# Second layer norm of a sequence-mixing and feed-forward kernel: epsilon on GpSimd, ten of sixteen normalizations as one ScalarE pass, under a new written order

## The chip, the cores and the metric

The kernel runs on one core of a Trainium2 chip. A core has five instruction queues that run side by side and wait for each other through semaphores: PE (TensorE, matrix products and transposes), DVE (VectorE), ACT (ScalarE), POOL (GpSimd) and SP (SyncE, which here only issues DMAs). PEld is TensorE's loading of weights. Each queue works strictly in its own order: an instruction that waits holds up all that stands behind it on the same engine.

The metric is the device time of one execution in microseconds (us). The profile tells of the span, from the first to the last instruction, which is a little shorter.

## The reference

The input x is 2048 tokens by 640 channels. The first half is a long convolution with gates, around the normalized x; the second is a feed-forward block with the Mish activation on the normalized result of the first.

```python
x = A_q
h  = x + _A_ref(_layernorm(x), A_k, A_v, A_shift_k, A_ssm_k, A_ssm_D)
h2 = h + _B_ref(_layernorm(h), B_w1, B_b1, B_w2)

# _A_ref(q, k, v, ...):
#   k_shift = causal convolution of k with 4 taps per channel
#   kv      = k_shift * v
#   y       = causal convolution of kv with ssm_k (2048 taps per channel, by FFT) + kv * ssm_D
#   return q * y
# _B_ref(x, w1, b1, w2):           # 640 -> 1728 -> 640
#   hid = x @ w1 + b1
#   return (hid * tanh(softplus(hid))) @ w2
```

`_layernorm` subtracts the mean over the 640 channels and divides by the root of the variance plus 1e-5.

## The kernel before, in words

The long convolution is done as a transform in two stages written as matrix products. The work is cut into named operations, and each stage writes a PSUM buffer (there are four of them, `ps0` to `ps3`) which ACT or DVE then evicts, that is copies to SBUF as bf16:

- `d_n`, `d_k`, `d_v`, `d_g`, `d_x`: loads of the filter, k, v, the table G and x (q), in pieces. `dadd` adds `ssm_D` to the filter's first tap.
- `k1pe`/`k1ev`: transposes of the filter; `s1kpe`/`s1kev`: first stage of the transform of the filter, 20 tiles; `s2kpe`/`s2kev`: second stage, 22 tiles.
- `ktpe`/`ktev`/`ktsh`: transposes of k and a shift by one; `kspe`: the four-tap convolution, ten tiles; `kv`: the product with v, on DVE from PSUM.
- `s1v`, `s2v`: the two stages for kv. `sw`: a copy of the filter's transform with pairs of partitions swapped, by DMA. `pr`: product of both transforms on DVE, 20 pieces.
- `i1pe`/`i1ev`: first inverse stage, 20 tiles; `i2a`, `i2b`, `i2pe`: second inverse stage, one tile of 128 tokens each (16 tiles), evicted by `y`.

Then each of the 16 token tiles goes through the gate and the two layer norms:

- `ln1_` (DVE, lines 506 to 510): statistics of x; `ln1p` (POOL): epsilon, power -0.5 and minus mean times that; `lnx` (ACT or POOL): the normalized x in one pass.
- `wb` (DVE): y times the normalized x; `h` (DVE): plus x, in place.
- `bn` (DVE, lines 540 to 545): statistics of h, and in a last small instruction the variance plus epsilon (`ve2`, line 544); `pow` (POOL, line 546): `ve2` to the power -0.5, `r2`; `hc` (DVE, lines 547 and 548): h minus mean, times `r2`, one instruction over 128 by 640.
- `tr`: the transpose of hc into the layout of the feed-forward block: on PE for tiles 0 and 1 (`trpe`, evicted by `trev`), by a transposing DMA on SP's queue for the others.

The feed-forward block works on units of 2, 2, 4, 4 and 4 token tiles. `m1pe{unit}_{0..6}` are the first products (line 586, and 593 for the last half chunk), `hb` the Mish pass on ACT (line 608), `m2pe` the second products (line 651), `res` the addition of h (DVE, line 676), `d_out` the store on SP's queue. Units 0 and 1 share their second products, which wait for all their `hb`.

The order of the operations on every queue is not found at run time: it is the text `ORDER` (lines 26 to 61), emitted token by token. `@2` says which PSUM buffer an operation of PE writes, `:a`, `:d` and `:p` override the engine (ACT, DVE, POOL). An operation of PE that takes a PSUM buffer waits until the eviction of its last user is done. All DMAs marked as loads, swaps, transposes and stores stand on SP's queue in this order too.

Of the kernel before, what the change touches and what calls it, by code (L numbers as in the profile page):

```python
# [30 lines left out]
ktpe4_1 ktpe1_0@0 ktpe1_1 ktpe1_3 d_g3 ktpe1_2 ktpe4_2 ktev1:a ktpe0_0@2 ktev4 ktpe0_2 ktpe0_1 ktpe2_0@1 d_g0 ktpe0_3 ktpe2_2 ktev0 s1kpe4_3@3 d_g5
s1kpe4_1@0 s1kev4_3 ktpe2_3 s1kev4_1:d ktsh0 ktpe3_0@2 ktpe3_1 d_g6 ktsh1 ktpe3_3 ktpe3_2 ktpe2_1 ktsh4 ktev3 kspe0_0@3 ktev2:a wsh1 d_g4 kspe0_1@0
kv0_0 s1kpe2_3@2 s1kpe4_2@1 kv0_1 s1kev2_3 ktsh3 kspe4_1@3 ktsh2 s1kev4_2 s1kpe3_1@2 kv4_1 s1vpe0_2@0 s1kev3_1 s1kpe2_1@1 s1vev0_2:d s1vpe0_1@3
s1kev2_1 kspe1_1@2 s1vev0_1 s2kpe_36@0 kv1_1 s2kpe_114@1 s2kev_36 kspe3_0@3 s2kev_114:d s2kpe_24@2 kspe1_0@0 s2kev_24 kv3_0 s2kpe_18@1 s2kpe_12@2
s2kev_18 kv1_0 kspe4_0@3 s2kev_12 s2kpe_90@1 kv4_0 s2kpe_54@0 s2kev_90 kspe3_1@2 s2kev_54 s2kpe_60@3 kv3_1 s1vpe0_3@1 s2kev_60 s2kpe_78@0 kspe2_1@2
s1vev0_3 s2kev_78:d s2kpe_102@3 s2kpe_0@1 kv2_1 s2kev_102 kspe2_0@0 s2kev_0 s2kpe_66@3 d_x3 kv2_0 s1vpe1_3@2 s2kev_66 s1vpe3_2@1 s1vev1_3:d d_x1
s1vpe3_0@0 s1vev3_2 s1vpe1_1@3 d_x0 d_x2 s1vev3_0 s1vev1_1:d s1vpe0_0@2 s2kpe_120@1 s1vev0_0 s1vpe2_2@0 s2kev_120:d s1vpe1_2@3 s1vev2_2 s1vpe2_0@2
s1vev1_2:d s1vpe1_0@1 s1vev2_0 s2kpe_6@0 d_t2m s2kpe_72@3 s1vev1_0 s2kev_6:d s2kpe_48@2 s2kev_72 s2kpe_96@1 s2kev_48:d s2v0pe_16@0 s2kev_96 s2kpe_84@3
s2v0ev_16:d s2kpe_30@2 s2kev_84 s1vpe4_2@1 ln1_3 s2kev_30 s2kpe_42@0 s2kpe_126@3 s2kev_42 s2kev_126:d s2kpe_108@2 ln1p3 ln1_0 s1vpe4_1@3 s2kev_108
s1vpe4_0@0 s1vev4_1:d s1vev4_2 ln1p0 s1vpe4_3@2 sw0_0 sw0_1 s1vev4_0 s1vev4_3:d s1vpe2_3@1 sw3_0 s1vpe3_3@3 lnx3:p s1vev2_3 sw1_1 s1vpe3_1@0  # L40
s1vev3_3:d s1vpe2_1@2 sw4_1 s1vev3_1 s2v0pe_0@1 lnx0:p sw2_1 ln1_1 s2v0pe_96@3 s1vev2_1 sw1_0 s2v0pe_80@0 sw3_1 ln1_2 s2v0ev_96 ln1p1 s2v0pe_64@2
sw2_0 s2v0ev_80 s2v0ev_0:d sw4_0 s2v0pe_32@3 lnx1:p s2v0ev_64 s2v0pe_112@0 pr0_0 ln1p2 s2v0pe_48@1 s2v0ev_112 s2v2pe_0@2 s2v0ev_32:d lnx2:p s2v0ev_48
s2v2pe_112@0 pr0_64 s2v2ev_112 s2v2pe_80@3 s2v1pe_64@1 s2v2ev_0 pr0_96 s2v2ev_80 s2v2pe_96@0 pr0_32 s2v2pe_32@2 s2v2ev_96 s2v2pe_64@3 pr1_96 s2v2ev_64
s2v2pe_16@0 pr1_64 s2v2ev_32 i1pe0_0@3 s2v1ev_64 s2v2pe_48@2 pr1_32 s2v2ev_48 i1pe0_3@1 pr1_0 s2v2ev_16 s2v1pe_0@2 pr3_32 i1ev0_0 s2v1pe_96@0 i1ev0_3
pr3_96 s2v1pe_32@3 s2v1ev_0 pr3_64 i1pe0_2@1 d_w12 s2v1ev_32 d_w11 i1pe0_1@2 pr4_96 d_w10 i1ev0_2 d_w13 i1pe1_2@3 pr3_0 d_w14 i1ev0_1 i1pe1_3@1
i1ev1_2 pr2_64 i1pe1_0@2 s2v1ev_96 pr2_0 i1pe3_0@3 i1ev1_3 i1pe3_2@0 pr2_32 i1ev1_0 i1pe3_1@1 pr4_64 i1ev3_0 i1pe3_3@2 i1ev3_1 pr2_96 i1pe1_1@3
# [4 lines left out]
hc2 pow3 y9 m1pe0_1@0 ln1_12 tr2 y5 w2z hb0_0 m1pe0_4@1 hc3 wb9 ln1p5 tr3 hb0_1 wb4 m1pe0_2@2 hb0_4 ln1_11 ln1p8 lnx5 m1pe0_5@3 wb7 hb0_2 ln1p12
ln1_10 m1pe0_6@0 hb0_5 m1pe1_6@1 h4 ln1p11 lnx12 ln1_15 m1pe1_0@2 hb1_6 ln1p10 ln1_14 lnx11 m1pe1_3@3 bn4 hb0_6 ln1p15 hb1_0 m1pe1_5@1 hb1_3 wb5
m1pe1_2@0 h7 hb1_5 wb6 h6 m1pe1_4@2 lnx15:p hb1_2 bn7 pow4 m1pe1_1@3 hb1_4 h5 pow7 hc4 i2pe11@1 bn6 hb1_1 ln1p14 tr4 i2pe12@0 m2pe0@2 y12 h9 lnx14:p
hc7 lnx10 bn9 pow6 y11 lnx8 hc6 pow9 bn5 tr6 m2pe2@3 wb14 pow5 tr7 hc9 wb10 wb11 tr9 wb8 hc5 h10 tr5 h8 wb15 bn8 m2pe1@0 h11 pow8 bn10 hc8 pow10 res0
m1pe2_6@1 h15 d_out0 ln1_13 tr8 m1pe2_1@2 hc10 ln1p13 hb2_6 res2 tr10 bn11 lnx13:p m1pe2_3@3 h14 hb2_1 pow11 wb12 hc11 h12 tr11 bn15 m2pe3@1 hb2_3
d_out2 wb13 pow15 bn14 hc15 pow14 bn12 tr15 m1pe3_6@2 h13 pow12 bn13 m1pe2_0@3 hc14 pow13 hb3_6 res3 res1 d_out3 hc12 d_out1 m1pe2_4@1 hc13 tr14 hb2_0
tr13 m1pe3_4@2 hb2_4 tr12 m1pe2_2@0 hb3_4 m1pe3_1@3 hb2_2 m1pe3_5@1 hb3_1 m1pe2_5@2 m1pe3_3@0 hb2_5 m1pe3_0@3 hb3_3 hb3_5 m1pe3_2@2 hb3_0 m2pe5@0
hb3_2 m2pe7@1 m2pe4@3 res7 res5 d_out7 d_out5 m2pe6@2 m1pe4_0@1 res6 res4 d_out4 d_out6 m1pe4_2@0 hb4_0 m1pe4_6@2 m1pe4_1@3 hb4_6 hb4_2 m1pe4_3@1
# [110 lines left out]
def kernel(  # L169
# [333 lines left out]
    for t in range(NT):  # L503
# [36 lines left out]
        def bnf(e, t=t):  # L540
            for hh in range(2):
                nc.vector.bn_stats(st2[:, t, hh, :], xt(t)[:, hh * 320:(hh + 1) * 320])  # L542
            nc.vector.bn_aggr(mv2[:, t, :], st2[:, t, :, :])
            nc.vector.tensor_scalar(ve2[:, t:t + 1], mv2[:, t, 1:2], EPS, None, ALU.add)  # L544
# [1 line left out]
        o_pw = OP(f"pow{t}", "pool", [o_bn, o_small], emit=lambda e, t=t: nc.gpsimd.tensor_tensor(r2[:, t:t + 1], ve2[:, t:t + 1], mhalf[:], ALU.pow))  # L546
        o_hc = OP(f"hc{t}", "dve", [o_pw] + ([trs[t - 7]] if t >= 7 else list(ks_pes.values())),
                  emit=lambda e, t=t: nc.vector.tensor_scalar(hc_s[t % 7], xt(t), mv2[:, t, 0:1], r2[:, t:t + 1], ALU.subtract, ALU.mult))
# [173 lines left out]
```

## Time and profile before

| | us |
|---|---|
| median of three executions | 226.48 (226.25 to 226.64) |
| profiled execution | 226.59 |
| its span | 224.7 |
| PE busy | 214.4 (95%) |
| DVE busy | 137.6 (61%) |
| ACT busy | 131.6 (59%) |
| POOL busy | 58.5 (26%) |

The busy shares are means over stages that differ: up to about 100 us, DVE and ACT are busy nearly all the time; from about 117 us on they have little to do, and PE has no gap. The granted clock of TensorE is full throughout. In the profile a line of the timeline gives the start, the duration, the engine, the source line, the operation, the tile written and the tiles read, how many in a row, and in brackets the idle time ahead of it and what ended that. `ks`, `uv`, `ra`, `rb`, `rw` and `G` are the big SBUF areas, which are used for several things one after another; `ps` is PSUM.

### The profile page before, as it was taken

What the parts mean: (1) busy time and instruction counts of PE and PEld (TensorE: products, weight loads), DVE (VectorE), ACT (ScalarE), POOL (GpSimd) and SP (SyncE); (2) the same over time, 40 slices, a digit from 0 to 9 for tenths busy, and PEclk for the clock granted to TensorE, in tenths of its full rate; (3) what the DMA queues carried; (4) which work ended last, traced back from release to release, by engine and by line L of the source; (5) the groups of instructions that cost most, each with busy time, mean ns of one, the idle gap of its engine ahead of it and who ended that gap; (6) DMA issues with size and microseconds to landing.
All of it is one profiled execution on the core that took longest, in us unless ns stands there. A gap on an engine that the chain in (4) does not pass through costs nothing.

```text
span 224.7 us, 6128 instructions
## 1 busy us (share of the span) xinstructions
PE 214.4 (95%) x2644; PEld 157.3 (70%) x2650; DVE 137.6 (61%) x250; ACT 131.6 (59%) x178; POOL 58.5 (26%) x106
## 2 busy tenths in 40 slices
...
GB/s 177 386 414 416 417 369 16 139 340 276 417 417 18 274 125 158 254 0 58 5 29 76 59 98 67 128 18 0 3 0 58 40 21 0 0 20 29 88 29 73
DMA packets 19563, 30.98 MB, mean 138 GB/s; under 512 B 10704, under 2 KB 14928, under 8 KB 18768
## 3 DMA queue, kind: packets, MB, share of 16 engines
...
q10 hardware_dynamic: 336, 0.12, 0.3%
...
## 4 chain that ended last, share of the span: by engine, by line
PE 65%; DVE 11%; ACT 10%; DMA 6%; POOL 3%; issue 2%; SPq 0%; DVEq 0%; POOLq 0%
PE ps L651 26%; PE ps L586 22%; ACT uv L259 8%; DVE ks L459 6%; DMA rb<-in_A_q_dram 4%; PE ps L394 3%; DMA ks<-in_A_ssm_k_dram 2%; PE ps L339 2%; PE ps L355 2%; PE ps L420 2%; PE ps L374 2%; PE ps L356 2%; PE ps L395 1%; PE ps L593 1%; PE ps L659 1%
## 5 line engine op out<-in xcount | busy, mean ns | idle before, releaser
L608 ACT ACTIVATE ks<-ps,b1s 128x512 bf16<-128x512 f32 (+1 forms) x69 | 36.2, 599 | 47.9 <-PE ps L586 30.7
L651 PE MATMUL ps<-ks 128*128 128x320 bf16 (+2 forms) x420 | 58.6, 299 | 0.0
L586 PE MATMUL ps<-G 128*128 128x512 bf16 (+1 forms) x319 | 57.5, 336 | 0.8 <-ACT ks L608 0.5
L651 PEld LDWEIGHTS <-ks 128*128 128x128 bf16 x420 | 40.6, 98 | 17.4 <-issue 1.3
L586 PEld LDWEIGHTS <-G 128*128 128x128 bf16 x325 | 31.2, 98 | 25.3 <-issue 1.3
L259 ACT CAST uv<-ps 128x1024 bf16<-128x1024 f32 x49 | 45.7, 1099 | 0.1
L676 DVE TENSOR_TENSOR rb<-ps,rb 128x640 bf16<-128x640 f32 x15 | 11.8, 820 | 50.5 <-PE ps L659 48.1
L259 ACT CAST ks<-ps 128x960 bf16<-128x960 f32 (+2 forms) x46 | 37.7, 912 | 7.9 <-PE ps L395 5.9
L459 DVE TENSOR_TENSOR ks<-ks,uv 128x2048 bf16<-128x2048 bf16 x20 | 23.4, 1239 | 0.0
L420 PEld LDWEIGHTS <-G 128*128 128x128 bf16 x512 | 20.6, 96 | 3.6 <-issue 2.9
L477 PE MATMUL ps<-a_t,ks 128*128 128x128 bf16 x320 | 19.0, 219 | 0.9 <-ACT uv L259 0.5
L477 PEld LDWEIGHTS <-ks 128*128 128x128 bf16 x320 | 18.4, 113 | 1.5 <-issue 0.5
L513 POOL TENSOR_SCALAR ve<-mv 128x1 f32<-128x1 f32 x16 | 4.6, 289 | 47.7 <-DVE mv L509 46.7
L546 POOL TENSOR_TENSOR r<-ve,mhalf 128x1 f32<-128x1 f32 x16 | 10.8, 675 | 16.9 <-DVE ve L544 16.8
L420 PE MATMUL ps<-uv,G 128*128 128x64 bf16 (+1 forms) x384 | 12.7, 186 | 1.7 <-ACT uv L259 1.3
L508 DVE BATCH_NORM_STATS2 st<-rb 128x6 f32<-128x320 bf16 x32 | 13.8, 472 | 0.8 <-DMA rb<-in_A_q_dram 0.8
L542 DVE BATCH_NORM_STATS2 st<-rb 128x6 f32<-128x320 bf16 x32 | 14.0, 480 | 0.1
L261 DVE CAST ks<-ps 128x1024 bf16<-128x1024 f32 (+2 forms) x12 | 13.2, 1127 | 1.4 <-PE ps L395 0.7
L261 DVE CAST uv<-ps 128x1024 bf16<-128x1024 f32 x11 | 13.1, 1205 | 0.1
L673 DVE TENSOR_TENSOR rb<-ps,rb 128x384 bf16<-128x384 f32 (+1 forms) x2 | 1.0, 492 | 19.9 <-PE ps L651 19.9
L360 DVE TENSOR_TENSOR ra<-ps,rb 128x1024 bf16<-128x1024 f32 x10 | 11.9, 1219 | 1.3 <-PE ps L356 0.7
L522 POOL TENSOR_SCALAR ra<-rb,r,nmr 128x640 bf16<-128x640 bf16 x10 | 12.1, 1212 | 1.2 <-PE ps L395 0.6
...
## 6 DMA issues: line engine op xcount, KB each, us to landing
...
```

Source lines behind the costliest of these rows:

```text
L259: nc.scalar.copy(o, i)
L261: nc.vector.tensor_copy(o, i)
L360: nc.vector.tensor_tensor(kv_w[:, m, :, 8 * h:8 * h + 8, :], p_.f32().rearrange("p (l t d) -> p d t l", l=4, t=8), raw_v[:, 8 * h:8 * h + ...
L420: nc.tensor.matmul(p_.f32()[:, o:o + n], g_v[:, f, :], src[:, :, f, :], start=True, stop=True)
L459: nc.vector.tensor_tensor(o, o, v, ALU.mult)
L477: nc.tensor.matmul(pz[:, dgl, :], KS[:, k, b, :, l], a12[:, k, :], start=k == 0, stop=k == 1)
L508: nc.vector.bn_stats(st1[:, t, hh, :], xt(t)[:, hh * 320:(hh + 1) * 320])
L522: nc.gpsimd.tensor_scalar(lnx_s[t % 9], xt(t), r1[:, t:t + 1], nmr1[:, t:t + 1], ALU.mult, ALU.add)
L542: nc.vector.bn_stats(st2[:, t, hh, :], xt(t)[:, hh * 320:(hh + 1) * 320])
L586: nc.tensor.matmul(ph[:, o:o + w], w1[:, dc, fc * P:fc * P + P], lt[:, dc, 0:w], start=dc == 0, stop=dc == NDC - 1)
L608: nc.scalar.activation(hb[:, fc, 0:n], p_.f32()[:, i * 512:i * 512 + n], ACT.Mish, bias=b1s[:, fc:fc + 1], scale=1.0)
L651: nc.tensor.matmul(p_.f32()[:, o:o + n], lhs, w2[:, k, cols:cols + n], start=fc == 0, stop=single and fc == 13)
```

## The change

In the second layer norm:

- the variance plus epsilon is computed by POOL, as the first instruction of `pow`, instead of by DVE as the last of `bn`;
- for ten tiles (3, 5, 7, 9, 10 to 15) `pow` gets a third instruction, minus mean times `r2` (`nmr2`), and `hc` becomes one ACT pass, scale times h plus bias, instead of the DVE instruction. Tiles 0, 1, 2, 4, 6 and 8 stay on DVE.

With this the whole text `ORDER` is replaced by another order of the same operations. What of it differs, as far as it is spoken of below:

- The filter's first stage (`s1k`) is complete before `kspe0_0`; then `kspe` and `s2k` alternate. Before, four `s1k` tiles and three `s1v` tiles stand among the `kspe`.
- `dadd1` and `dadd4` are on DVE instead of POOL; `ktev1` and `ktev2` are on DVE and `ktev4` on ACT, instead of the reverse.
- The loads of v are issued later, those of x begin with `d_x0` right after the first five products with v, and `ln1_0` stands among the last products; the table load `d_t2m` moves from behind the loads of x to behind the five loads of w1.
- Nine instead of ten `ln1_` stand ahead of the first y; `lnx7` is on ACT ahead of the y, `y1` is on DVE. Seven `lnx` instead of ten are on POOL.
- The order of the token tiles is another; `i2pe8` and `i2pe13` are the two that come behind the first feed-forward products, before it was 11 and 12. As before, 14 of the 16 come ahead of `m1pe0_3`, the first of them.
- At the end `m2pe14` is followed by `m2pe15b` alone; before, `m2pe13` stood between.

```diff
 ORDER = """
-d_dr wz idn d_n0 cz wm@0 small lane d_n1 d_cst d_sk d_n2 warm d_n4 d_n3 kz d_g7 dsel dcol dadd0 d_k0 k1pe0@1 dadd1:p d_k3 k1pe1@2 d_k1 k1ev0b d_k2
+d_dr wz idn d_n0 cz wm@0 small lane d_n1 d_cst d_sk d_n2 warm d_n4 d_n3 kz dsel d_g5 dcol dadd0 d_k0 k1pe0@1 dadd1 d_k2 k1pe1@2 d_k1 k1ev0 d_k3 k1ev0b
...
-i2a2@0 y0 i2b1 i2pe8@3 y1 wb0 i2pe4@2 h0 y8 i2pe14@1 wb1 y4 bn0 i2pe15@3 y14 i2b2 i2a3@2 y2 i2b3 h1 i2pe13@1 pow0 y3 bn1 i2pe6@0 lnx9:p y15 i2pe7@2
-y13 wb2 i2pe10@3 pow1 y7 hc0 i2pe9@1 h2 y6 trpe0@2 hc1 wb3 trev0:a trpe1@0 bn2 trev1:a i2pe5@2 y10 m1pe0_3@0 h3 pow2 lnx4 bn3 lnx7:p m1pe0_0@3 hb0_3
+d_w2a i2b1 lnx7 lnx6:p i2b0 i2a3@2 y1:d i2b3 i2pe11@1 y0 wb1 i2pe14@0 h1 y11 i2pe15@3 wb0 y14 bn1 i2pe12@1 y15 i2a2@0 y3 h0 i2b2 i2pe7@3 pow1 bn0 y2
+i2pe9@2 y7 i2pe10@0 wb3 pow0 y9 i2pe4@3 hc1 y12 h3 trpe1@2 y4 hc0 wb2 trpe0@1 trev1:a h2 i2pe6@3 trev0:a bn2 i2pe5@2 y10 m1pe0_3@1 bn3 y5 pow2 y6
+m1pe0_4@0 wb7 pow3 hb0_3 hc2 m1pe0_5@2 h7 tr2 wb4 w2z hc3 m1pe0_0@3 wb6 hb0_4 h4 ln1p11 tr3 bn4 m1pe0_6@1 hb0_0 m1pe0_2@0 lnx5 ln1_14 pow4 m1pe0_1@3
...
-d_out8 d_out11 m2pe14@3 m2pe13@0 res14 res12 d_out14 m2pe15b@1 res13 d_out13 d_out12 res15b d_out15b
+m2pe10@0 m2pe12@3 res10 res8 d_out10 d_out8 m2pe14@2 m2pe15b@0 res12 res14 d_out12 res15b d_out14 d_out15b
 """.split()
...
+HC_ACT = (3, 5, 7, 9, 10, 11, 12, 13, 14, 15)
...
+    nmr2 = cpool.tile([P, NT], F32, name="nmr2")
...
             nc.vector.bn_aggr(mv2[:, t, :], st2[:, t, :, :])
-            nc.vector.tensor_scalar(ve2[:, t:t + 1], mv2[:, t, 1:2], EPS, None, ALU.add)
         o_bn = OP(f"bn{t}", "dve", [o_h], emit=bnf)
-        o_pw = OP(f"pow{t}", "pool", [o_bn, o_small], emit=lambda e, t=t: nc.gpsimd.tensor_tensor(r2[:, t:t + 1], ve2[:, t:t + 1], mhalf[:], ALU.pow))
-        o_hc = OP(f"hc{t}", "dve", [o_pw] + ([trs[t - 7]] if t >= 7 else list(ks_pes.values())),
-                  emit=lambda e, t=t: nc.vector.tensor_scalar(hc_s[t % 7], xt(t), mv2[:, t, 0:1], r2[:, t:t + 1], ALU.subtract, ALU.mult))
+
+        def pwf(e, t=t):
+            nc.gpsimd.tensor_scalar(ve2[:, t:t + 1], mv2[:, t, 1:2], EPS, None, ALU.add)
+            nc.gpsimd.tensor_tensor(r2[:, t:t + 1], ve2[:, t:t + 1], mhalf[:], ALU.pow)
+            if t in HC_ACT:
+                nc.gpsimd.tensor_scalar(nmr2[:, t:t + 1], mv2[:, t, 0:1], r2[:, t:t + 1], -1.0, ALU.mult, ALU.mult)
+        o_pw = OP(f"pow{t}", "pool", [o_bn, o_small], emit=pwf)
+
+        def hcf(e, t=t):
+            if t in HC_ACT:
+                nc.scalar.activation(hc_s[t % 7], xt(t), ACT.Identity, bias=nmr2[:, t:t + 1], scale=r2[:, t:t + 1])
+            else:
+                nc.vector.tensor_scalar(hc_s[t % 7], xt(t), mv2[:, t, 0:1], r2[:, t:t + 1], ALU.subtract, ALU.mult)
+        o_hc = OP(f"hc{t}", "act" if t in HC_ACT else "dve", [o_pw] + ([trs[t - 7]] if t >= 7 else list(ks_pes.values())), emit=hcf)
```

More of the change, by code (lines that the diff above doesn't have):

```diff
@@ L31 @@
[L31 to L46, printed above, removed]
@@ L51 @@
[L51 to L58, printed above, removed]
@@ new lines @@
+ktpe2_0@0 ktsh4 ktpe2_3 d_g1 ktpe2_2 s1kev4_3 ktpe2_1 kspe0_0@3 ktev2 s2kpe_60@1 s2kpe_66@2 kv0_0 s2kev_60 ktsh2 kspe1_0@0 s2kev_66 s2kpe_54@1 kv1_0
+s2kpe_84@3 s2kev_54 kspe2_0@2 s2kev_84:d s2kpe_96@0 kspe3_0@1 s2kev_96 kv2_0 s2kpe_120@3 s2kpe_6@0 s2kev_120 kv3_0 kspe4_0@2 s2kev_6 s2kpe_48@3 kv4_0
+s2kpe_102@1 s2kev_48 kspe0_1@0 s2kev_102:d d_x0 s2kpe_78@2 d_x1 kspe2_1@3 s2kev_78 kv0_1 s2kpe_36@1 s2kpe_30@2 s2kev_36 kv2_1 kspe1_1@0 s2kev_30
+s1vpe0_1@1 kv1_1 s2kpe_18@3 s1vev0_1 s2kpe_108@2 ln1_0 kspe3_1@0 s2kev_18 s2kpe_72@1 s2kev_108 kv3_1 ln1p0 kspe4_1@3 s2kev_72 s1vpe0_2@2 kv4_1
@@ new lines @@
+d_w2a i2b1 lnx7 lnx6:p i2b0 i2a3@2 y1:d i2b3 i2pe11@1 y0 wb1 i2pe14@0 h1 y11 i2pe15@3 wb0 y14 bn1 i2pe12@1 y15 i2a2@0 y3 h0 i2b2 i2pe7@3 pow1 bn0 y2
+i2pe9@2 y7 i2pe10@0 wb3 pow0 y9 i2pe4@3 hc1 y12 h3 trpe1@2 y4 hc0 wb2 trpe0@1 trev1:a h2 i2pe6@3 trev0:a bn2 i2pe5@2 y10 m1pe0_3@1 bn3 y5 pow2 y6
+m1pe0_4@0 wb7 pow3 hb0_3 hc2 m1pe0_5@2 h7 tr2 wb4 w2z hc3 m1pe0_0@3 wb6 hb0_4 h4 ln1p11 tr3 bn4 m1pe0_6@1 hb0_0 m1pe0_2@0 lnx5 ln1_14 pow4 m1pe0_1@3
+hb0_5 ln1_10 ln1p14 m1pe1_5@2 hb0_1 hc4 wb5 ln1p10 hb0_6 tr4 m1pe1_0@3 ln1_9 hb1_5 lnx14 m1pe1_3@1 h5 ln1p9 h6 hb1_0 bn6 m1pe1_2@2 lnx10 lnx11:p bn7
```

30 lines of the change are left out of this document (24 added, 6 removed).

## The prediction

> **What bounds the kernel now.** I read the stretches first (busy time of each engine between two times), then the chain of waits, then each engine's timeline, then the spreads of single lines.
>
> ```profile
> 24.90:42.70 17.80, 17.80 (x377) 17.03 (x376) 16.18 (x15) 16.23 (x17) 3.40 (x4) 1.00 0.52 201
> ...
> 54.00:91.90 37.90, 35.05 (x788) 32.42 (x783) 37.60 (x50) 37.58 (x42) 15.19 (x26) 1.00 0.65 245
> 91.90:99.90 8.00, 7.67 (x60) 4.51 (x59) 7.36 (x22) 7.97 (x14) 2.81 (x5) 1.00 0.22 79
> 99.90:116.70 16.80, 16.28 (x150) 13.59 (x148) 14.97 (x45) 15.38 (x34) 14.08 (x28) 1.00 0.20 21
> 116.70:222.00 105.30, 104.72 (x670) 61.52 (x674) 34.16 (x83) 28.51 (x46) 10.33 (x16) 1.00 0.16 41
> ```
>
> The columns are start and end, length, then busy time of PE, PEld, DVE, ACT, POOL, the granted clock, the DMA share and GB/s. The clock is 1.00 throughout. From 25 to 43 us PE is never free; from 54 to 100 us ACT and DVE are full; from 116.7 us PE alone is full. So the end is set by when the feed-forward part starts, plus a PE-bound remainder.
>
> ```profile
> 53.50 38.07 ACT L259 CAST uv<-ps 128x1024 bf16<-128x1024 f32 x41
> ...
> 91.92 6.66 ACT L259 CAST ks<-ps 128x640 bf16<-128x640 f32 x11 [0.28 <-PE ps L529]
> 98.51 1.38 ACT L259 COPY G<-ps 128x640 bf16<-128x640 bf16 x2
> ```
> ```profile
> 98.22 0.44 DVE L548 TENSOR_SCALAR rw<-rb,mv,r 128x640 bf16<-128x640 bf16 x1
> ```
> ```profile
> 99.94 7.31 PE L586 MATMUL ps<-G 128*128 128x256 bf16 x65
> ...
> 107.78 0.71 PE L586 MATMUL ps<-G 128*128 128x256 bf16 x5 [0.52 <-ACT ks L608]
> ...
> 116.73 7.23 PE L651 MATMUL ps<-ks 128*128 128x320 bf16 x52
> ```
>
> ACT works without a gap from 53.50 to 91.57 us: 41 evictions, 0.93 us each. Then come eleven y at 0.61 us and the two transposed tiles (trev0, trev1), and at 99.94 us the first m1pe starts; call this moment M. DVE reaches M together with ACT: hc1 ends at 98.66 us, 1.28 us before M. Behind M only 0.52 us of PE is lost before m2pe0 at 116.73 us, and almost nothing after. Profiled execution 226.59 us, span 224.7: 1.89 us lie around it. It is 0.11 us above the median, 226.48.
>
> **The change, part by part.** The diff also replaces the whole written order, so I count what each engine has ahead of M.
>
> *ACT ahead of M.* One more eviction of s2k, one kt copy less (ktev1 and ktev2 go to DVE, ktev4 comes), one y less (y1 goes to DVE), and lnx7 is new here.
>
> ```profile
> 20.67 1.87 ACT L259 COPY uv<-ps 128x2048 bf16<-128x2048 bf16 x1 [0.86 <-PE ps L339]
> ...
> 34.59 4.41 ACT L259 CAST ks<-ps 128x960 bf16<-128x960 f32 x5 [0.25 <-PE ps L420]
> ...
> 108.81 0.92 ACT L520 ACTIVATE ra<-rb,nmr,r 128x640 bf16<-128x640 bf16 x1 [0.42 <-POOL nmr L515]
> 109.64 0.82 ACT L608 ACTIVATE ks<-ps,b1s 128x256 bf16<-128x256 f32 x2
> ```
>
> +0.88 (4.41/5) -1.87 -0.61 +0.83 (109.64-108.81) = -0.77 us.
>
> *DVE ahead of hc0 (now the second of the two).* One set of first-norm statistics less (ln1 nine times instead of ten), two epsilon additions less, one s2k eviction less, one kt copy more, y1 more, two additions to the raw filter more (dadd1, dadd4 come from GpSimd).
>
> ```profile
> 20.98 2.42 DVE L261 COPY uv<-ps 128x2048 bf16<-128x2048 bf16 x2 [0.65 <-PE ps L339]
> ...
> 47.60 2.22 DVE L261 CAST ks<-ps 128x960 bf16<-128x960 f32 x2 [0.19 <-PE ps L420]
> ...
> 86.17 0.83 DVE L508 BATCH_NORM_STATS2 st<-rb 128x6 f32<-128x320 bf16 x2
> ...
> 87.17 0.83 DVE L508 BATCH_NORM_STATS2 st<-rb 128x6 f32<-128x320 bf16 x2
> ...
> 92.72 0.49 DVE L536 TENSOR_TENSOR ks<-ks,ra 128x640 bf16<-128x640 bf16 x1 [0.36 <-ACT ks L259]
> ...
> 95.21 0.15 DVE L544 TENSOR_SCALAR ve<-mv 128x1 f32<-128x1 f32 x1
> 95.28 0.48 DVE L538 TENSOR_TENSOR rb<-ks,rb 128x640 bf16<-128x640 bf16 x1
> ```
>
> -1.00 (87.17-86.17) -2x0.07 (95.28-95.21) -1.11 +1.21 +0.75 (y1: an estimate between the 1.11 for 960 columns and the 0.49 for 640 columns without PSUM) +0.3 = 0.0. But the 0.36 us that DVE waits for ACT's first y goes, since y1 is DVE's own: -0.36.
>
> *The chain of one tile.* Today DVE adds epsilon and GpSimd raises to the power; now GpSimd does both, and a third step for the ten ACT tiles.
>
> ```profile
> 86.34 0.22 POOL L513 TENSOR_SCALAR ve<-mv 128x1 f32<-128x1 f32 x1 [19.24 <-DVE mv L509]
> 86.65 0.57 POOL L514 TENSOR_TENSOR r<-ve,mhalf 128x1 f32<-128x1 f32 x1
> 87.33 0.26 POOL L515 TENSOR_SCALAR nmr<-mv,r 128x1 f32<-128x1 f32 x1
> ...
> 95.45 0.72 POOL L546 TENSOR_TENSOR r<-ve,mhalf 128x1 f32<-128x1 f32 x1 [2.96 <-DVE ve L544]
> ```
>
> Today, from the epsilon's start at 95.21 to the power's end at 96.17: 0.96 us. Then: 86.34 to 87.22 = 0.88 us for two steps, 1.25 for three. Nothing lost on tiles 0 and 1, +0.3 on an ACT tile, and its pass costs 0.83 on ACT instead of 0.35 of DVE. Sixteen epsilons (4.9 us with gaps) and ten third steps (3.7) come to GpSimd, three lnx leave it; it is free for 2.7 of the 16.8 us behind M, where most of this falls, so there it is filled.
>
> *Before 43 us.* The new order does all s1k first and then feeds PE with kspe and s2k in turn. I walked it by hand with the pitches of the rows (kspe 0.78 us, s2k 0.42, s1 0.45, k1 1.16, kt 1.02 on PE; 0.88 to 0.95 per ACT eviction, 1.17 per product of k and v on DVE).
>
> ```profile
> 24.98 0.06 PE ps L355
> ...
> 41.36 0.06 PE ps L356
> ```
>
> Today's chain lies on PE from kspe0_0 (24.98) to kspe2_0 (ends 41.42): ten kspe 7.8, eleven s2k 4.6, four s1k 1.8 and three s1v 1.35 are 15.6 us of work in 16.4. In the new order the stretch from kspe0_0 to s1vpe0_2 has ten kspe, fifteen s2k, two s1v: 15.0 us. Up to it the old order does 18.1 us of PE work by 24.98, the new one 19.9 before kspe0_0. Without a hand-off lost it would start that stretch at about 26.6 us and be through at 42.0, with 34.9 us of PE work against the old 33.7 at 41.4 and about 34.3 at 42.0: a lead of up to 0.6 us. If it loses as many hand-offs as today, 0. The other side: dadd1 now stands in DVE's queue ahead of k1ev0 and waits for the filter's second load.
>
> ```profile
> 6.42 1.29 DVE L261 COPY ks<-ps 128x1024 bf16<-128x1024 bf16 x2 [0.98 <-PE ps L374]
> ```
> ```profile
> 7.03 0.30 POOL L368 TENSOR_SCALAR ks<-ks,dcol 128x1 bf16<-128x1 bf16 x1 [2.71 <-DMA ks<-in_A_ssm_k_dram]
> ```
>
> That holds k1ev0 from 6.42 to 7.2 us: 0.8 us, covered while PE transposes k1pe1 (till 8.05); without this cover +0.8. I take a lead of 0.3, ends -0.6 and +0.8.
>
> *M.* ACT: -0.77 -0.3 = -1.1. DVE: -0.36 -0.3 = -0.7. The later one decides: M moves by -0.7, to 99.2 us.
>
> *From M to m2pe0.* As many Mish passes and y; on ACT lnx5, lnx14, lnx10 and hc3 instead of lnx4, lnx5, lnx12 and lnx11. hc3 waits for bn3, which DVE ends some 1.8 us behind M (bn2 and bn3, 1.0 each, stand behind hc0 and h2), and for three GpSimd steps of 1.25: it can start at M+3.2 and lets hb0_4 free its bank at M+4.9, just when PE has come to m1pe0_2. Cover nil, but no wait: PE's 0.52 shrinks to about 0.2: -0.3, ends -0.5 and +1.2.
>
> *After m2pe0.* The later hc passes are on ACT, which is busy 28.5 of 105.3 us there. Unit 2 needs tile 5's transpose at about M+27; hc5 stands on ACT behind y13 (i2pe13 is ready at M+16.5), two lnx and hc7, 0.83 each, and would end at M+20. 0, ends 0 and +0.5. The transposes stay in SP's queue behind d_out0 and d_out2, which wait for m2pe2 and precede tr9, tr10 and tr8; unit 3 needs them at M+40, I see them by M+35.
>
> ```profile
> 72.66 2.23 SPq L323 DMA_DIRECT2D G<-in_B_w_dram  x5
> ```
> ```profile
> ra<-tab_t2m SPq DMA_DIRECT2D x1, 1024.0 KB, 8.5
> ```
>
> The t2m load moves on SP's queue behind ten swaps and these five loads of w1, to about 75 us. With its 8.5 us from issue to landing it is there at 83.5, and the first i2 reads it ten evictions of y ahead of M, at about 90: covered by 6 us.
>
> *Tail.* res12 and res14 now fall into the 1.5 us of m2pe15b, instead of one addition.
>
> ```profile
> 216.34 1.56 DVE L676 TENSOR_TENSOR rb<-ps,rb 128x640 bf16<-128x640 f32 x2 [5.93 <-PE ps L659]
> ...
> 220.25 0.82 DVE L676 TENSOR_TENSOR rb<-ps,rb 128x640 bf16<-128x640 f32 x1 [2.35 <-PE ps L651]
> ...
> 221.78 0.43 DVE L673 TENSOR_TENSOR rb<-ps,rb 128x256 bf16<-128x256 f32 x1 [0.70 <-PE ps L651]
> ```
>
> Two take 1.56 us where 1.53 are free (220.25 to 221.78): +0.1, ends 0 and +0.3.
>
> Sum: -0.7 -0.3 +0.1 = -0.9: 226.59 becomes 225.7, or 225.6 against the median.
>
> **Rivals.** *GpSimd late for hc3.* Lines vary when DVE runs beside them:
>
> ```profile
> L513 POOL TENSOR_SCALAR ve<-mv x16: 208/222/1062, 52.9 to 129.6; 128x1 f32<-128x1 f32 x16
> ```
> ```profile
> L515 POOL TENSOR_SCALAR nmr<-mv,r x16: 254/259/603, 53.9 to 130.7; 128x1 f32<-128x1 f32 x16
> ```
>
> With the longest of each, 1.06+0.72+0.60 instead of 1.25, hc3 and PE come 1.1 us later: 226.7, no change. For it speaks GpSimd's full stretch; against it, that the medians sit at the short end. The Trainium skill, page "SBUF — State Buffer", section "Who interferes with whom", says that a VectorE instruction with two SBUF inputs and a GpSimd one that reads SBUF exclude each other for the whole instruction; by that rule each of the three steps can wait for one wb or h. The spread above agrees in kind, though the medians show that it is rare.
>
> *The statistics meet a late load (slower).* ln1_0 now stands among the last products on DVE, needed at 39.5 us; its load goes out when the fifth product is done, about 35.0.
>
> ```profile
> DMA to landing us min/median/max: 4.2/4.2/4.2
> ```
> ```profile
> 43.08 8.60 DMA rb<-in_A_q_dram
> ```
>
> The first of the four q loads landed after 4.2 us, the third after 8.6. First in line it lands at 39.2, in time by 0.3. If it takes 3 us more, DVE stands for 2.7, its two last products and M with it: 228.3. From 1.7 us of lateness on it decides for slower. Against it: here it is first.
>
> *Lost hand-offs where ACT now has none.* A wait of ACT for PE is 0.2 to 0.3 us (rows above); six more between 43 and 92 us make +1.5: 227.1, slower. For it: PE is at 35.1 of 37.9 us there. Against: both orders ask the same PE work per eviction.
>
> *No lead, or dadd1's wait uncovered.* M moves by -0.4 to +0.4: 225.9 to 226.7, about no change.
>
> **How the numbers follow.** Two executions cannot be told apart below about 0.2%, 0.45 us. Forecast 225.6 (own range 224.9 to 226.0): 0.52. No lead or dadd1: 0.12; GpSimd late: 0.10; both about the same time. Late load: 0.12; lost hand-offs: 0.14. So faster 0.52, same 0.22, slower 0.26. The range leaves out the late load and the best corner of the bounds: 224.7 to 227.3.
>
> **What would show it.** Right: M at 98.8 to 99.5 us, ACT without gaps from 54 to 92, m2pe0 16.3 to 16.8 us behind M, PE full to the end. Wrong: a DMA wait at DVE's first ln1 statistics; ACT waiting on nmr ahead of hc3 and PE behind it; PE waits between 25 and 43 us; or m1pe2 waiting for a transpose.

## The result, and the profile after

The changed kernel takes 228.07 us (median of 14 executions, 227.37 to 229.91), the kernel before 226.56 (14 executions beside it, 226.05 to 227.25). The ratio is 1.0074 (95% interval 1.0050 to 1.0097): slower by 0.7%, where 225.6 was forecast. The executions of the changed kernel fall into two groups: nine between 227.37 and 228.14 us at a granted clock of 1.00, and five between 228.98 and 229.91 at 0.992 or 0.993. The profiled one, 229.0 us with a span of 227.1, is of the second group.

In after the helper's eviction line is L261, the first products L598, Mish L620, hc L557 on ACT and L559 on DVE, GpSimd's steps L549 (epsilon), L550 (power) and L552 (minus mean times that), and the transpose L573. PE's timeline of after, around M:

```profile
98.71 5.08 PE L598 MATMUL ps<-G 128*128 128x256 bf16 x45
104.06 2.34 PE L598 MATMUL ps<-G 128*128 128x256 bf16 x20 [0.27 <-ACT ks L620]
108.58 7.73 PE L598 MATMUL ps<-G 128*128 128x256 bf16 x55 [2.18 <-DMA G<-rw]
...
119.09 3.15 PE L663 MATMUL ps<-ks 128*128 128x320 bf16 x22
```

M is at 98.71 us, 1.23 earlier than before. But m2pe0 stands at 119.09, 20.38 us behind M, where it was 16.79. The new row is the third: PE stands for 2.18 us ahead of m1pe1_5, the first product that needs tiles 2 and 3, and waits for a transpose by DMA.

The stretches of after (columns as in the prediction):

```profile
54.00:90.30 36.30, 33.34 (x755) 31.35 (x752) 35.65 (x47) 36.30 (x42) 9.38 (x20) 1.00 0.81 300
...
98.70:119.10 20.40, 17.95 (x152) 14.47 (x150) 17.63 (x52) 15.33 (x35) 16.48 (x40) 0.92 0.17 33
106.40:108.58 2.18, 0.00 (x1) 0.03 (x1) 2.15 (x7) 1.20 (x3) 1.81 (x5) 0.96 0.38 75
108.58:112.00 3.42, 3.42 (x18) 2.48 (x19) 3.28 (x11) 1.09 (x3) 2.99 (x8) 0.53 0.00 0
119.10:224.50 105.40, 104.63 (x669) 61.48 (x673) 26.96 (x56) 38.12 (x58) 9.92 (x25) 1.00 0.16 39
```

ACT is full from 54 to 90.3 us, as forecast. Right behind PE's pause the granted clock is 0.53 for 3.4 us. The Trainium skill, page "TensorE: Matmul & The Clock Gate", section "Part 1: The HAM clock gate (the "warmup" mystery)", gives a free-running window of 3413 ns and a half clock after an idle one; the length agrees with the trace, but here the pause ahead of it was only 2.18 us.

The chain of waits of after shows what the 2.18 us consist of:

```profile
100.45 0.35 POOL ve L549
100.80 0.07 issue
100.87 0.62 POOL r L550
...
101.64 0.70 POOL nmr L552
102.34 0.03 issue
102.36 0.92 ACT rw L557
...
103.31 5.14 DMA G<-rw
```

hc3 starts at 102.36, M+3.65 (before, on DVE, it was over at M+3.8), and then tile 3's transpose takes 5.14 us to land. The times of all transposes, issue to landing, stand in one row for each kernel; before:

```profile
DMA to landing us min/median/max: 2.4/2.4/4.8
```

and after:

```profile
DMA to landing us min/median/max: 2.6/2.6/5.1
```

A transpose reports in 16 parts, which the trace has one by one. In after, 15 parts of tile 3 are there at 106.61 to 106.73 us, and the last at 108.44. Between them lies one packet of another queue. The DMA queues of after, from 105.5 to 107.4 us:

```profile
q8 instruction: 1, 0.02, 5.0%
q1 hardware_dynamic: 15, 0.00, 1.8%
```

This packet of 16 KB starts at 105.62 and takes 1.51 us. A transpose moves its data as 672 packets of queue 1. All but two of tile 3's have started by 105.84 us; from 105.9 to 107.1 no packet starts, and from 107.1 to 107.3 us these do:

```profile
q1 hardware_dynamic: 2, 0.00, 1.4%
```

They start at 107.11 and 107.12, as the packet of queue 8 ends (107.13). Queue 8 has 21 packets of 16 KB in the whole profile, and PE has 5,314 instructions, 253 to each: it brings PE's program. (The Trainium skill, page "Runtime: NRT & Kernel Launch", section "Instruction fetch mechanics", says that each engine's program comes in blocks of 16 KiB, 256 instructions, by a DMA queue of the engine's own. The count here agrees.) In before a packet at 104.65 did the same to tile 2: 15 parts at 104.78 to 104.89, the last at 107.19. There PE came to its first product with tiles 2 and 3 at 107.26 us and lost 0.52. Another instruction queue, 14, has a packet of 8 KB near by (105.12 us, 0.31 us long in after); in fetch_early2 below it falls, at 107.12 us, among tile 3's data (106.41 to 107.77), and no part is held.

So theory 1: PE's code packet meets tile 3's transpose and holds back its last part; PE pauses, and in some executions the clock halves. Theory 2: hc3, with three GpSimd steps ahead of its pass on ACT, is late by itself.

### The profile page after: what moved, and what is told of

The parts are those of the page before. It is cut to its first block, busy times and chain, and to the rows that moved or that the text cites. A ratio compares the mean times of both kernels' runs of the same rounds, so it can differ in the third digit from the quotient of the medians.

```text
span 227.1 us, 6129 instructions
## 1 busy us (share of the span) xinstructions
PE 215.7 (95%) x2643; PEld 158.7 (70%) x2650; DVE 132.3 (58%) x227; ACT 140.3 (62%) x190; POOL 57.4 (25%) x127
## 4 chain that ended last, share of the span: by engine, by line
PE 66%; DVE 12%; ACT 8%; DMA 5%; POOL 4%; issue 3%; SPq 0%; POOLq 0%; DVEq 0%
PE ps L663 25%; PE ps L598 23%; ACT uv L261 8%; PE ps L396 3%; PE ps L422 3%; DVE ks L461 3%; PE ps L341 2%; DMA ks<-in_A_ssm_k_dram 2%; DMA G<-rw 2%; DVE ks L263 2%; DVE uv L263 2%; PE ps L376 2%; PE ps L357 2%; DVE st L544 1%; PE ps L397 1%
## 5 line engine op out<-in xcount | busy, mean ns | idle before, releaser
L598 PE MATMUL ps<-G 128*128 128x512 bf16 (+1 forms) x318 | 59.3, 343 | 2.8 <-DMA G<-rw 2.2
L620 ACT ACTIVATE ks<-ps,b1s 128x512 bf16<-128x512 f32 (+1 forms) x69 | 35.9, 599 | 37.9 <-PE ps L598 32.4
L598 PEld LDWEIGHTS <-G 128*128 128x128 bf16 x325 | 31.9, 100 | 28.0 <-issue 4.5
L261 ACT CAST uv<-ps 128x1024 bf16<-128x1024 f32 x49 | 45.4, 1170 | 0.0
L261 ACT CAST ks<-ps 128x960 bf16<-128x960 f32 (+2 forms) x46 | 38.6, 922 | 7.9 <-PE ps L397 5.1
L461 DVE TENSOR_TENSOR ks<-ks,uv 128x2048 bf16<-128x2048 bf16 x20 | 22.9, 1216 | 0.1
L422 PEld LDWEIGHTS <-G 128*128 128x128 bf16 x512 | 20.7, 96 | 3.2 <-issue 2.5
L263 DVE CAST ks<-ps 128x1024 bf16<-128x1024 f32 (+3 forms) x12 | 12.9, 1098 | 0.9 <-PE ps L531 0.6
L557 ACT ACTIVATE rw<-rb,nmr,r 128x640 bf16<-128x640 bf16 x10 | 9.1, 922 | 5.2 <-POOL nmr L552 5.1
L422 PE MATMUL ps<-ks,G 128*128 128x160 bf16 x128 | 11.0, 230 | 0.1
L396 PE MATMUL ps<-cst,ra 128*64 128x128 bf16 x160 | 10.5, 219 | 0.3 <-DVE uv L263 0.2
```

What stands on the lines that cost most here:

```text
L261: nc.scalar.copy(o, i)
L263: nc.vector.tensor_copy(o, i)
L396: nc.tensor.matmul(ps[0:64, dgl, :], lhs, mc, start=True, stop=True)
L422: nc.tensor.matmul(p_.f32()[:, o:o + n], g_v[:, f, :], src[:, :, f, :], start=True, stop=True)
L461: nc.vector.tensor_tensor(o, o, v, ALU.mult)
L598: nc.tensor.matmul(ph[:, o:o + w], w1[:, dc, fc * P:fc * P + P], lt[:, dc, 0:w], start=dc == 0, stop=dc == NDC - 1)
```

## The experiments

From m2pe0's first matmul to the end of m2pe15b's last it is 105.01 us in every kernel profiled, before, after and the twelve below. All differences lie ahead, in M and in the distance from M to m2pe0. Times in us; "15 / last" is when tile 3's 15th and last part landed, behind its issue; the packet is the one of queue 8 nearest to the transposes.

| kernel | median | ratio to before, interval | M | M to m2pe0 | packet | tile 3: issue, 15 / last |
|---|---|---|---|---|---|---|
| before | 226.56 | | 99.94 | 16.79 | 104.65 | 103.83, +3.8 / +3.8 |
| after | 228.07 | 1.0050 to 1.0097 | 98.71 | 20.38 | 105.62 | 103.31, +3.4 / +5.1 |
| fetch_early | 229.14 | 1.0065 to 1.0143 | 102.33 | 17.22 | 102.12 | 106.93, +3.5 / +3.5 |
| fetch_early2 | 227.84 | 1.0043 to 1.0105 | 100.64 | 17.16 | 101.60 | 105.24, +3.5 / +3.5 |
| before_fetch_early2 | 227.13 | 1.0016 to 1.0042 | 100.94 | 16.11 | 101.84 | 104.84, +3.1 / +3.1 |
| pe_kept_busy | 227.66 | 1.0017 to 1.0058 | 99.18 | 18.75 | 105.92 | 103.78, +3.4 / +5.1 |
| hb04_first | 226.73 | 0.9976 to 1.0017 | 98.72 | 17.33 | 103.31 | 103.31, +3.6 / +3.7 |
| hc3_dve | 225.67 | 0.9935 to 0.9979 | 98.92 | 16.67 | 103.67 | 102.73, +3.6 / +3.8 |
| tile3_on_pe | 226.09 | 0.9949 to 0.9986 | 98.88 | 17.03 | 105.30 | none |
| hc3_dve_pe | 225.08 | 0.9912 to 0.9953 | 98.70 | 16.33 | 103.44 | none |
| hb04_first_pe | 225.74 | 0.9941 to 0.9971 | 99.39 | 16.60 | 105.22 | none |
| order_only | 227.23 | 1.0015 to 1.0045 | 99.09 | 17.51 | 103.94 | 103.55, +4.0 / +4.0 |
| order_eps | 225.85 | 0.9950 to 0.9981 | 98.84 | 17.13 | 103.45 | 102.64, +3.4 / +4.2 |
| ops_only | 226.59 | 0.9990 to 1.0016 | 100.44 | 16.62 | 105.12 | 105.38, +2.6 / +2.6 |

**The packet moved away: fetch_early and fetch_early2.** PE's program gets more instructions at its start, so that each later packet falls due earlier.

```diff
-        for _ in range(WARM):
-            nc.tensor.matmul(wm_p.f32()[:, 0:512], wz[:, 0:P], wz[:, P:D], start=True, stop=True)
+        for _ in range(60):
+            nc.tensor.matmul(wm_p.f32()[:, 0:64], wz[:, 0:P], wz[:, P:P + 64], start=True, stop=True)
```

> Kernel after, with the nine warm-up matmuls of 512 columns replaced by sixty of 64 columns: 51 matmuls (102 instructions with their weight loads) more in PE's program ahead of everything, no other change. Theory 1 (code packet): in the trace of after, 15 of the 16 completions of tile 3's transpose come at 106.6 to 106.7 us and the last at 108.44, and one instruction packet of 16 KB occupies one DMA engine from 105.6 to 107.1; its queue has 21 packets, which is PE's program of 5314 instructions at 256 each. With 51 matmuls more ahead, the same packet falls due some 5 us earlier, before any transpose is issued: tile 3's transpose lands 2.4 to 3.0 us after its issue, PE's wait of 2.18 us goes to 0.4 or less, the clock stays at 1.00, from the first feed-forward matmul to m2pe0 it is 16.3 to 17.0 us, time 225.2 to 226.0. Theory 2 (hc3 simply comes too late through three GpSimd steps): nothing changes, 227.4 to 229.9, the wait stays at about 2 us.

The stage answered, the kernel did not: M to m2pe0 fell from 20.38 to 17.22 us (16.3 to 17.0 were expected), but M came 3.6 us later. The reason for half of it stands in the stretch from 6.9 to 10.4 us, fetch_early:

```profile
6.90:10.40 3.50, 3.50 (x47) 3.20 (x47) 2.71 (x4) 0.37 (x1) 0.30 (x1) 1.00 1.01 396
```

and after:

```profile
6.90:10.40 3.50, 3.50 (x96) 3.30 (x96) 3.30 (x5) 1.75 (x2) 0.30 (x1) 1.00 1.01 391
```

47 matmuls against 96 in the same busy 3.5 us: half the clock. (The clock column has no record that early in fetch_early; its first, at 10.5 us, is of the full clock. In after that is at 6.0.) So the warm-up was repeated with 48 matmuls of 96 columns, the old 4,608 columns in all.

> Kernel after with the warm-up as 48 matmuls of 96 columns (the same 4608 columns, so that PE has no pause in it): 39 matmuls more in PE's program. In the run with sixty of 64 columns the granted clock came up at 10.5 us instead of 6.0 and the start of the feed-forward part moved by 3.6 us; here it should come up near 6 us. Theory 1 (code packet on tile 3's transpose): the packet falls at 100 to 102 us or so, ahead of the transposes' data; the 16th completion of tile 3's transpose comes with the other fifteen, PE waits 0.6 us or less, the clock holds, from the first feed-forward matmul to m2pe0 it is 16.6 to 17.3 us (20.4 in after), time 225.4 to 226.5. Theory 2 (hc3's lateness alone): 227.4 to 229.9.

PE's timeline of fetch_early2 around M:

```profile
100.64 5.08 PE L598 MATMUL ps<-G 128*128 128x256 bf16 x45
105.99 2.34 PE L598 MATMUL ps<-G 128*128 128x256 bf16 x20 [0.27 <-ACT ks L620]
108.85 6.17 PE L598 MATMUL ps<-G 128*128 128x256 bf16 x55 [0.52 <-DMA G<-rw]
...
117.80 4.37 PE L663 MATMUL ps<-ks 128*128 128x320 bf16 x31
```

With the packet at 101.60, tile 3's last part lands with the other fifteen; the wait is 0.52 instead of 2.18 us and the clock holds in this execution. (One of fetch_early2's eight executions, 230.28 us, and one of fetch_early's six, 230.88, show 0.993.) 17.16 us from M to m2pe0 is theory 1's number. hc3 is as late as in after (M+3.65), so its lateness is worth at most the 0.52 and the 0.27 that are left. The time of the whole kernel missed the forecast, since M moved by 1.93 us. Most of that is one row near 20 us in PE's timeline, a wait for nothing but PE's own next instruction:

```profile
20.05 0.22 PE L396 MATMUL ps<-cst,ks 128*64 128x128 bf16 x1 [1.41 <-issue]
```

A packet of code had started at 17.64. That PE ran out of instructions there is an inference; after has no such wait.

**The same shift in before: before_fetch_early2.**

> Kernel before with the same warm-up of 48 matmuls of 96 columns. In before the packet (104.65 us) held the 16th completion of tile 2's transpose from 104.9 to 107.2, and PE waited only 0.8 us or less for it. Theory 1: both transposes land within 3.5 us of their issue, time 225.9 to 226.5, so that before gains 0.1 to 0.6 and the change is worth about 0.5 once the packet is out of the way of both. Rival: the smaller matmuls of the warm-up help or hurt by themselves; then before moves by as much as after does.

M to m2pe0 fell from 16.79 to 16.11 us. Before's wait of 0.52 us ahead of m1pe1_6 is gone; PE's timeline has 70 products in one row:

```profile
100.94 7.86 PE L586 MATMUL ps<-G 128*128 128x256 bf16 x70
```

So before too had paid for the packet. But it has a wait for issue of 1.1 us near 20 us as well and came out slower, 227.13 us, where 225.9 to 226.5 were expected. With the packet out of the way in both, the stage takes 17.16 us with the change and 16.11 without: its new order and its hc3 cost 1.05 us there even so. Moving packets by padding is no cure.

**The pause filled: pe_kept_busy.** Twenty matmuls more, whose result is overwritten, stand where PE waits.

```diff
+                def kp(e, p_=p_):
+                    for i in range(20):
+                        nc.tensor.matmul(p_.f32()[:, 0:256], w1[:, i % NDC, 0:P], lt_s[0][:, i % NDC, 0:256], start=True, stop=True)
+                OP("keep", "pe", [lt_ready[0], lt_ready[1]] + d_w1, psum=p_, emit=kp)
...
-m1pe1_5@2 hb0_1
+keep@2 m1pe1_5 hb0_1
```

> Kernel after with twenty matmuls whose result is overwritten put on PE right ahead of unit 1's first product, in the place where PE waits 2.18 us for tile 3's transpose; they need only tiles 0 and 1. They fill that wait (20 x 0.11 = 2.2 us) and move nothing that waits for the transpose. Theory 1: the wait costs about 2 us and PE's idleness there is what halves the granted clock for 3.4 us in some runs (another 1.5 us). Then all runs here stand together at clock 1.00 and 227.3 to 227.8, and none at 229. Rival: the clock falls for another reason (the load of the whole part that follows); then about a third of the runs still stands at 229 with a clock of 0.992.

PE's timeline of pe_kept_busy:

```profile
106.79 2.34 PE L610 MATMUL ps<-G 128*128 128x256 bf16 x20
108.97 6.17 PE L598 MATMUL ps<-G 128*128 128x256 bf16 x55
...
117.93 4.24 PE L669 MATMUL ps<-ks 128*128 128x320 bf16 x30
```

The transpose lands as late as in after (+5.1), but the same 55 matmuls take 6.17 us instead of 7.73, and all twelve executions lie between 227.28 and 228.33 (four of them above the expected 227.8) at a clock of 0.998 or more. None of twelve executions without the pause shows the lower clock, five of fourteen with it do, and in after's profile it lies right behind the pause: so the pause is most likely what halves the clock. That costs 1.6 us in a third of after's executions.

**The packet moved by one exchange: hb04_first.**

```diff
-hc3 m1pe0_0@3 wb6 hb0_4
+hb0_4 hc3 m1pe0_0@3 wb6
```

> Kernel after with one exchange in ScalarE's order: the Mish passes of the second product (hb0_4) ahead of tile 3's normalization (hc3) instead of behind it. ScalarE waits 1.30 us for hc3's input anyhow; hb0_4 (0.85 us) fits into that wait, hc3 and the issue of tile 3's transpose stay where they are (103.3 us), and PE loses its 0.27 us wait for hb0_4's bank. Theory 1a (that short wait of PE holds back the fetch of its next code, which then meets tile 3's transpose): the code packet falls near 103.7 us instead of 105.6, as with hc3 on VectorE; the 16th completion of tile 3's transpose comes with the other fifteen, at 106.7 to 107.2; PE waits 0.4 to 1.0 us; from the first feed-forward matmul to m2pe0 16.6 to 17.3 us; time 225.5 to 226.4. Theory 1b (the packet's time has nothing to do with that wait): packet at 105.3 to 105.6, transpose at 108.4, 227.2 to 229.9 as after. Theory 2 (hc3's lateness): as 1b.

ACT's and PE's timelines of hb04_first:

```profile
102.36 0.92 ACT L557 ACTIVATE rw<-rb,nmr,r 128x640 bf16<-128x640 bf16 x1 [0.42 <-POOL nmr L552]
```
```profile
98.72 7.26 PE L598 MATMUL ps<-G 128*128 128x256 bf16 x65
107.09 6.16 PE L598 MATMUL ps<-G 128*128 128x256 bf16 x55 [1.12 <-DMA G<-rw]
...
116.05 2.20 PE L663 MATMUL ps<-ks 128*128 128x320 bf16 x15
```

hc3 and both issues stand where they stood in after, to the hundredth. But PE runs through its 65 matmuls, the packet comes at 103.31 instead of 105.62 and now holds the last part of tile 2 (106.55, the others by 103.78), and tile 3 is complete at 106.96. That is theory 1a's picture: the 0.27 us in which PE waited for a bank had pushed its code fetch by 2.3 us onto tile 3. The other kernels without padding agree. The packet starts 4.6 to 4.9 us behind M in the seven where PE's rows show no wait up to there (before, hb04_first, hc3_dve, hc3_dve_pe, order_only, order_eps, ops_only) and 6.4 to 6.9 us behind M in the three with that wait (after, pe_kept_busy, tile3_on_pe). In hb04_first_pe, where the transpose of tile 3 on PE waits for hc3, it is 5.8. The median falls by 1.3 us, to 226.73; the execution profiled, 225.85 us, is the fastest of the twelve. PE's wait of 1.12 us and the median are somewhat above the forecast: PE is there 0.4 us earlier than in after (105.97 against 106.40), and tile 3 still takes 3.7 us to land.

**Tile 3 taken off the detour, off the DMA, and both: hc3_dve, tile3_on_pe, hc3_dve_pe.**

```diff
-HC_ACT = (3, 5, 7, 9, 10, 11, 12, 13, 14, 15)
+HC_ACT = (5, 7, 9, 10, 11, 12, 13, 14, 15)
```
```diff
-        if t < PE_TILES:
+        if t in (0, 1, 3):
...
-tr3 bn4 m1pe0_6@1 hb0_0 m1pe0_2@0 lnx5 ln1_14 pow4 m1pe0_1@3 hb0_5 ln1_10
+trpe3@1 bn4 hb0_0 m1pe0_2@0 trev3:d lnx5 ln1_14 pow4 m1pe0_1@3 hb0_5 m1pe0_6@1 ln1_10
```

> Kernel after with tile 3's normalization back on VectorE (3 taken out of the set of ScalarE tiles; its third GpSimd step goes with it). Tile 3's transpose is issued about 1 us earlier, at 102.3 instead of 103.3 us. Theory 1 (code packet): the transpose is through before the packet at 105.6 and lands by 105.0; PE does not wait for it, clock 1.00, time 225.2 to 226.0, all of the 2.2 us gone for 1 us of earliness. Theory 2 (lateness alone, a transpose that takes 5.1 us): it lands at 107.4, PE still waits 1.1 us, time 226.4 to 227.0.

> Kernel after with tile 3 transposed on PE and copied out by VectorE, like tiles 0 and 1, instead of by a DMA; on PE it stands behind unit 0's fourth product. hc3 ends at 103.3 us as before, PE transposes by 103.9, VectorE copies by 104.8. Both theories: no wait for tile 3 any more, PE has 0.5 us more and VectorE 0.7 us more to do. Theory 1 and 2: from the first feed-forward matmul to m2pe0 17.0 to 17.5 us, clock 1.00, time 225.6 to 226.4. If the loss has its cause elsewhere (in the order behind, or in GpSimd's load), 227 or more.

> Both single mendings together: tile 3's normalization on VectorE and its transpose on PE. With hc3 on VectorE alone PE still waits 0.46 us for the transpose; here that wait goes, but PE transposes for 0.45 us and VectorE copies for 0.7. Expected about the same as the better of the two, 225.4 to 226.0; below 225.3 if the code packet on tile 2's transpose still cost something, above 226.1 if VectorE is now too late.

PE's timeline of hc3_dve:

```profile
98.92 7.26 PE L598 MATMUL ps<-G 128*128 128x256 bf16 x65
106.64 6.17 PE L598 MATMUL ps<-G 128*128 128x256 bf16 x55 [0.46 <-DMA G<-rw]
...
115.59 6.68 PE L663 MATMUL ps<-ks 128*128 128x320 bf16 x48
```

and of hc3_dve_pe:

```profile
98.70 4.53 PE L598 MATMUL ps<-G 128*128 128x256 bf16 x40
103.06 0.44 PE L569 MATMUL ps<-ident,rw 128*128 128x128 bf16 x5
103.34 8.90 PE L598 MATMUL ps<-G 128*128 128x256 bf16 x80
...
115.03 3.15 PE L663 MATMUL ps<-ks 128*128 128x320 bf16 x22
```

One tile put back on DVE turns 228.07 into 225.67: the issue comes 0.6 us earlier and the landing 1.9. By theory 2, 1.1 us of PE's wait would have been left; 0.46 was. hc3_dve did not hit theory 1's picture whole: the packet came earlier too (103.67), met tile 2, and tile 3 landed at 106.50, not 105.0. tile3_on_pe came out as both theories had it: 17.03 us from M to m2pe0 and 226.09 us, with hc3 as late as in after. So nothing behind that transpose makes the loss. With both edits nothing on PE waits from M to m2pe0, and 225.08 us, 0.67% below before, is the fastest of all these kernels; it lies under the 225.3 that stood for a packet that had still cost something in hc3_dve.

**The change kept, the transpose mended: hb04_first_pe** (both edits shown above).

> Kernel after with hb0_4 ahead of hc3 on ScalarE and tile 3 transposed on PE: the ten normalizations on ScalarE and epsilon on GpSimd stay as the change has them. PE meets neither the wait for hb0_4's bank (0.27 us) nor a transpose by DMA for tile 3. If the change itself is sound and the transposes' landing is all that spoilt it: from the first feed-forward matmul to m2pe0 16.4 to 16.8 us, as with hc3 on VectorE (16.33 there), time 225.0 to 225.7, the forecast of 225.6. If tile 3's pass on ScalarE costs something beside the transpose's time of issue: 225.9 to 226.3, as with the transpose on PE alone (226.09).

16.60 us from M to m2pe0 as expected; the time, 225.74, is a hair above its range because M is at 99.39. All ten ACT tiles are kept, and it beats before by 0.3 to 0.6%. What spoilt the change is tile 3's way through the DMA more than the passes on ACT. Whether hc3 on ACT costs something besides is open: hc3_dve_pe, with hc3 on DVE, is 0.27 us shorter from M to m2pe0 and 0.66 us in the median, and in the profiles M differs by 0.69 as well (98.70 against 99.39).

**Order and operations apart: order_only, ops_only, order_eps.** The new order with the old operations; the old order with the new ones; the new order with epsilon on GpSimd and all hc on DVE.

```diff
-HC_ACT = (3, 5, 7, 9, 10, 11, 12, 13, 14, 15)
+HC_ACT = ()
```

> The new order with the operations of before: epsilon on VectorE, all normalizations on VectorE as one pass. VectorE has two epsilons more ahead of the start of the feed-forward part (0.15 us) and tile 3's pass ends near 101.9 us there, so its transpose is issued about 1 us earlier than in after. Theory 1: no wait for tile 3 over 0.6 us, clock 1.00, time 225.4 to 226.2: the order alone is the gain that was forecast. Theory 2, and a loss made by the order: 226.5 to 228.

> The order of before with the operations of after: epsilon on GpSimd, ten normalizations on ScalarE. hc3 now stands on ScalarE behind hb0_0 and waits for three GpSimd steps. Theory 1 and 2: tile 3's transpose is issued 1 to 2 us later than the 103.8 us of before, PE waits 1 to 2.5 us for it, the clock may halve; time 227.2 to 229.5. If the three steps and the pass on ScalarE cost nothing in themselves, 226.3 to 226.9.

> The new order with epsilon on GpSimd and all sixteen normalizations on VectorE: it stands between the order alone (227.23) and the kernel with nine tiles on ScalarE (225.67). If epsilon's way to GpSimd is what gained, 225.6 to 226.2; if the nine passes on ScalarE are, 226.8 to 227.3, and VectorE is still the one that comes late for tiles 2 and 3.

The diff shown is order_eps; order_only also puts epsilon back on DVE. order_only fell into the range that stood for a loss made by the order (+0.3% to before), ops_only into the one for operations that cost nothing. In order_only's profile (226.76 us) the packet at 103.94 lies in the middle of tile 2's transpose, whose sixteen parts all land 4.9 to 5.1 us after issue, tile 3 follows at 107.5, and PE waits 1.30 us; why its median is 0.5 us above its profile was not settled. In ops_only hc3 on ACT is as late as expected (tile 3 issued at 105.38), but the packet (105.12 to 106.43) is over before that transpose's data start at 106.56; it lands in 2.6 us, and PE waits 0.36. In the new order epsilon on GpSimd gains: 227.23 to 225.85, with intervals apart. How much of that is GpSimd's doing and how much the transposes' is not separated, since tile 2 takes 5.1 us to land in order_only and 4.3 in order_eps. The nine ACT passes of hc3_dve add nothing that the intervals could tell (225.85 to 225.67).

## Why the prediction was wrong

- *M: right that it comes earlier, but not term by term.* Forecast 99.2 us (98.8 to 99.5), measured 98.71, a little ahead of that range, and 98.70 to 99.39 in the seven other kernels with the same operations ahead of it. ACT has no gap from 54.48 to 90.3 us. DVE, which was to decide, ends hc0 at 97.28 us, 1.38 ahead of hc1 in before instead of 0.7. The 0.36 us that it waits for its first y did not go; the row in after has 0.62:

```profile
90.76 0.82 DVE L263 CAST ks<-ps 128x640 bf16<-128x640 f32 x1 [0.62 <-PE ps L531]
```

  Of the gain that made up for it, 0.5 us is the lead with which DVE ends its last product of both transforms (84.72 instead of 85.22 us), where 0.3 was taken. The rest was not taken apart.
- *From M to m2pe0: this step failed.* It said -0.3, ends -0.5 and +1.2; measured +3.59. Its working followed hc3 to the bank that hb0_4 frees, and that part held: hc3 began at M+3.65 against M+3.2, and PE lost 0.27 us against 0.2. But it ended there. hc3 is also what tile 3's transpose waits for, and m1pe1_5 waits for that. The sum had no term for it, though the list of signs of a failure had "ACT waiting on nmr ahead of hc3 and PE behind it". In the trace: 1.71 us for the held last part (106.73 to 108.44), about 0.5 that remains of the wait when the packet is away (0.52 in fetch_early2), and 1.6 for the halved clock (7.73 against 6.17 us). With the 0.27, and less the 0.52 that before loses, that is 3.5 of the 3.59 us.
- *The 0.52 us that this step started from was misread.* The profile puts before's wait ahead of m1pe1_6 down to ACT, and the prediction took it for hb0_4's bank. But hb0_4 is the last of the six passes in this row of before's ACT timeline and ends at 105.50:

```profile
103.17 2.33 ACT L608 ACTIVATE ks<-ps,b1s 128x256 bf16<-128x256 f32 x6
```

  PE stood until 107.78 us. Tile 2's transpose landed at 107.19 and tile 3's at 107.64; an ACT pass for another bank happened to end at about that time. The view of before's transposes (line 561) has the wait, on the loading of weights:

```profile
who waited for it (us, times):
  PEld L586: 0.8, 1
```

  And with the packet out of the way it is gone (before_fetch_early2). So the one wait that the prediction found between M and m2pe0, and meant to shrink, was already a wait for transposes.
- *After m2pe0: right at 0.* 105.01 us in both.
- *Tail: +0.1, measured 0.* The last addition of after starts 105.05 us behind m2pe0 (224.14 less 119.09), as in before (221.78 less 116.73). DVE's timeline at the end of after:

```profile
222.50 1.56 DVE L688 TENSOR_TENSOR rb<-ps,rb 128x640 bf16<-128x640 f32 x2 [5.98 <-PE ps L671]
224.14 0.42 DVE L685 TENSOR_TENSOR rb<-ps,rb 128x256 bf16<-128x256 f32 x1
```

- *The rivals.* The late load did not come: the load landed at 39.47 us, 4.1 behind its issue, and ln1_0 starts at 39.75, behind its predecessor on DVE, without a wait. No hand-offs were lost for ACT between 54 and 90 us. GpSimd was late for hc3: its three steps took 1.87 us (100.45 to 102.32) instead of 1.25, and the row for it is

```profile
101.59 0.73 POOL L552 TENSOR_SCALAR nmr<-mv,r 128x1 f32<-128x1 f32 x1
```

  against 0.26 elsewhere, while DVE ran two products and began an addition, each of two SBUF inputs. That agrees with the rule cited in the prediction. But this rival was priced by ACT's and PE's bank alone, 1.1 us, and none of the rivals had a transpose, a code packet or the clock in it. Slower had 0.26, for other mechanisms; the time lies above the range's end of 227.3.

In sum, against the profiled execution: M gave 0.5 us more than forecast, M to m2pe0 took 3.9 more, the tail 0.1 less; 225.7 becomes 229.0.
